# Attention scores: one product over 128 rows and 144 columns, or two products over 64 rows and 72 columns each

## The chip, the cores and the metric

The kernel runs on one core of a Trainium2 chip. The metric is the device time of one execution in microseconds, median of three. For the kernel before that is 1152.58 us (1152.16 to 1152.69).

## The reference

The program is pooled attention, then a dense mixture of four experts, then a gated block. Only the scores of the attention change; they are the product in the fifth line below.

```
q, k, v: (4 batches, 8 heads, 576 tokens, 64 dims)
k_p = k.reshape(B, H, 72, 8, D).mean(axis=3)          # 72 pooled keys per head
v_p = v.reshape(B, H, 72, 8, D).mean(axis=3)
scale = 1 / sqrt(64)
scores = scale * q @ k_p.T                            # per head: 576 x 64 by 64 x 72
attn = softmax(scores, axis=-1)                       # the kernel adds 1e-9 to the sum, as the reference does
x = attn @ v_p
x -> (2304, 512); out = sum over 4 experts of p_e * relu(x @ w1_e) @ w2_e
a, b = out @ g_w1, out @ g_w2;  result = ((a * b) @ g_w3) @ g_wout
```

## The kernel before

The 2304 tokens are cut into 18 tiles of 128, and three tiles make a block of 384. A batch has 576 tokens, so tile 4 and tile 13 lie across the border of two batches; `segments` cuts those two into halves of 64 tokens, and the other sixteen are whole.

Attention runs for each tile in steps written out by hand. `make_qT` turns q so that the 128 partitions hold the 64 dims of an even head and the 64 dims of the odd head next to it; there are four such pairs. `make_kT` turns the pooled keys the same way. To keep the two heads of a pair apart, the pooled keys are spread over twice the columns: a pair has 144 columns, the first 72 nonzero only in the even head's 64 rows, the last 72 only in the odd head's (the mask `mk` in `pool_k`). `scores` multiplies qT (the stationary operand, 128 rows by 128 tokens) with these 144 columns, pair by pair, so half of what TensorE multiplies is zero. Two PSUM banks take a tile: pairs 0 and 1 in the first, pairs 2 and 3 in the second. The data is f32, and one matmul of the program stands in the trace as two passes, each with its own weight load; a whole tile is 4 matmuls and 8 passes.

`exps` then takes one bank after the other: a maximum on VectorE (L516), a subtraction on VectorE (L522) and the exponential on ScalarE (L523). For the first two tiles it is instead a scaling on VectorE (L518) and one exponential per head on ScalarE (L520). `sums` and `normalise` follow, `attn_T` transposes the result on TensorE (L543), and `attend` (L558) multiplies with the pooled values into x, where the two heads of a pair go to output partitions 0 to 63 and 64 to 127.

Tiles 0 to 2 are done in a lead of fixed order, in which nothing else is there for TensorE. Tiles 3 to 17 are hooks between the units of the first expert (`g`, L174 to L176, three passes over 384 or 512 columns each). In that part the attention's steps share two PSUM banks in turn (`spare[:2]`): scores, transposes of the keys and of the probabilities, and the first two pairs of `attend`. A step waits until ScalarE and VectorE have read what was in the bank before. [...] After 181 us no attention is left.

Of the kernel before, what the change touches and what calls it, by code (L numbers as in the profile page):

```python
# [17 lines left out]
def fused_kernel(  # L18
# [16 lines left out]
    nc = tc.nc  # L35
    PSUM = bass.MemoryType.PSUM

    B, H, S, D = q.shape
    POOL = 8
    NK = S // POOL  # L40
    NT, DM = out.shape
    E, _, F = moe_w1.shape
    P = 128
# [10 lines left out]
    NP = H // 2  # L54
# [6 lines left out]
    def segments(t0, n):  # L61
        done = 0
        while done < n:
            b, s = divmod(t0 + done, S)
            step = min(n - done, S - s)
            yield done, step, b, s
            done += step
# [263 lines left out]
    with tc.manual_schedule():  # L331
# [16 lines left out]
        def bank(name):  # L348
            turn[0] += 1
            return spare[(turn[0] - 1) % len(spare)](name)  # L350
# [46 lines left out]
        in_t, kb_t, kT_t, vp_t, qT_t, sc_t, e_t, sm_t, at_t = {}, {}, {}, {}, {}, {}, {}, {}, {}  # L397
# [96 lines left out]
        W = 2 * NK  # L494
        G = H // 2

        def scores(t):
            qT = qT_t.pop(t)
            sc_t[t] = []
            for half in range(2):  # L500
                sc = bank("sc")
                for hp in range(2 * half, 2 * half + 2):
                    for off, n, b, s in segments(t * P, P):
                        nc.tensor.matmul(sc[off:off + n, (hp % 2) * W:(hp % 2 + 1) * W],  # L504
                                         qT[:, hp, off:off + n], kT_t[b][:, hp * W:(hp + 1) * W],
                                         start=True, stop=True)
                sc_t[t].append(sc)

        def exps(t):
            e = ap.tile([P, H, NK], F32, tag="e", name="e", bufs=3)  # L510
            mx = ap.tile([P, H], F32, tag="mx", name="mx")
            for half, sc in enumerate(sc_t.pop(t)):
                s3 = sc[:, :2 * W].rearrange("p (g j) -> p g j", j=NK)
                m = mx[:, half * G:(half + 1) * G]
                eh = e[:, half * G:(half + 1) * G]
                nc.vector.tensor_reduce(m, s3, axis=AX.X, op=ALU.max)  # L516
                if t < LEAD - 1:
                    nc.vector.tensor_scalar(m, m, -LOGIT, None, op0=ALU.mult)  # L518
                    for g in range(G):
                        nc.scalar.activation(eh[:, g], s3[:, g], AF.Exp, scale=LOGIT, bias=m[:, g:g + 1])  # L520
                else:
                    nc.vector.tensor_tensor(eh, s3, m.unsqueeze(2).broadcast_to([P, G, NK]), op=ALU.subtract)  # L522
                    nc.scalar.activation(eh, eh, AF.Exp, scale=LOGIT)  # L523
            e_t[t] = e
# [75 lines left out]
        def do_scores(t):  # L600
            return [(None, lambda: scores(t))]

        def do_exps(t):
            return [(None, lambda: exps(t))]
# [887 lines left out]
```

## Time and profile before

| | |
|---|---|
| median of 3 runs | 1152.58 us |
| the profiled execution's own time | 1151.8 us |
| its span, first to last instruction | 1150.0 us |
| TensorE busy | 1138.5 us, 99% |
| weight loads busy | 1031.7 us, 90% |
| VectorE busy | 795.9 us, 69% |
[...]

The chain that ended last is read backwards from the last instruction and says which engine's work fills the time. In the rows below, PE is TensorE's matmuls and PEld its weight loads. Matmuls are pipelined: a matmul row's own duration holds latency that the next one overlaps, so the cost of a pass is the distance from one start to the next, which the chain's rows give directly. "x8" means eight records merged into one row.

### The profile page before, as it was taken

How to read it: one execution, taken by the hardware profiler on the slowest of the kernel's cores; microseconds unless marked ns; L12 is line 12 of the kernel's file. 1: busy time of each engine (PE TensorE's matmuls, PEld its weight loads, DVE VectorE, ACT ScalarE, POOL GpSimd, SP SyncE). 2: the span in 40 equal slices, each digit the busy share in tenths (PEclk: the TensorE clock that was granted, in tenths of full speed). 3: DMA queues.
4: the chain of work that ended last, by engine and by line, in shares of the span. 5: the costliest groups of instructions: out<-in, count | busy, mean ns of one | idle time of the engine just before them, and what ended most of it. 6: DMA issues, size and time to landing. Idle time of an engine off the chain costs nothing.

```text
span 1150.0 us, 17113 instructions
## 1 busy us (share of the span) xinstructions
PE 1138.5 (99%) x5966; PEld 1031.7 (90%) x5966; DVE 795.9 (69%) x1464; ACT 369.8 (32%) x615; POOL 422.3 (37%) x393
## 2 busy tenths in 40 slices
PE   7999999999999999999999999999999999999998
PEld 6898888999989898989898989989889999999997
DVE  6867553767858598658689677877786675774554
ACT  4543433345413053504134421305353223230110
POOL 6974312423615156634335652515000111331211
PEclk9999999999999999999999999999999999999999
DMA  9865525345785825495954677785486075947341
GB/s 214 210 154 136 164 89 201 138 178 179 273 271 168 263 78 161 131 311 172 268 157 129 192 233 188 236 212 139 151 192 236 33 270 201 334 156 282 116 166 55
DMA packets 213766, 213.85 MB, mean 186 GB/s; under 512 B 88880, under 2 KB 169008, under 8 KB 213680
## 3 DMA queue, kind: packets, MB, share of 16 engines
q1 hardware_dynamic: 213392, 212.23, 59.7%
q8 instruction: 47, 0.77, 0.3%
q10 hardware_dynamic: 288, 0.52, 0.1%
q14 instruction: 39, 0.32, 0.1%
HBM read 140.87 MB, written 71.83 MB: 185 GB/s over the span
## 4 chain that ended last, share of the span: by engine, by line
PE 98%; DVE 1%; ACT 0%; issue 0%; DMA 0%; POOL 0%; DVEq 0%; ACTq 0%
PE g L176 18%; PE g L174 18%; PE g L175 18%; PE s L176 13%; PE s L174 13%; PE s L175 13%; PE sc L504 1%; PE x_ps L558 1%; PE at_ps L543 1%; DMA stxh<-in_k_dram 0%; DVE ap L419 0%; PE vp_ps L452 0%; PE kT_ps L432 0%; PE qT_ps L483 0%; ACT ap L520 0%
## 5 line engine op out<-in xcount | busy, mean ns | idle before, releaser
L958 DVE TENSOR_TENSOR plain<-s,plain 128x384 f32<-128x384 f32 x300 | 158.4, 554 | 83.6 <-PE s L176 34.9
L180 POOL TENSOR_TENSOR round<-x5l,round 128x768 fp32r<-128x768 f32 x60 | 112.0, 1866 | 271.5 <-ACT round L179 245.1
L176 PE MATMUL s<-xo,wl 128*128 128x384 f32 x624 | 208.6, 334 | 0.0
L174 PE MATMUL s<-xo,wh 128*128 128x384 f32 x624 | 208.6, 334 | 0.0
L175 PE MATMUL s<-xo,wh 128*128 128x384 f32 x624 | 208.5, 334 | 0.0
L174 PE MATMUL g<-w2l,round 128*128 128x512 f32 x522 | 204.8, 392 | 0.0
L176 PE MATMUL g<-w2h,round 128*128 128x512 f32 x522 | 203.8, 390 | 0.0
L175 PE MATMUL g<-w2h,round 128*128 128x512 f32 x522 | 203.5, 390 | 0.0
L175 PEld LDWEIGHTS s<-xo,wh 128*128 128x128 f32 x624 | 117.1, 188 | 0.5
L174 PEld LDWEIGHTS s<-xo,wh 128*128 128x128 f32 x624 | 117.1, 188 | 0.5
L176 PEld LDWEIGHTS s<-xo,wl 128*128 128x128 f32 x624 | 117.1, 188 | 0.0
L176 PEld LDWEIGHTS g<-w2h,round 128*128 128x128 f32 x522 | 98.0, 188 | 20.6
L174 PEld LDWEIGHTS g<-w2l,round 128*128 128x128 f32 x522 | 98.1, 188 | 20.0 <-issue 0.8
L175 PEld LDWEIGHTS g<-w2h,round 128*128 128x128 f32 x522 | 98.0, 188 | 19.4
L292 POOL TENSOR_TENSOR x5l<-x5l,x5h 128x256 uint32<-128x256 uint32 x80 | 60.4, 755 | 137.7 <-DVE x5h L291 134.2
L962 ACT ACTIVATE plain<-s 128x384 f32<-128x384 f32 x60 | 29.2, 487 | 230.8 <-PE s L176 226.6
L179 ACT ACTIVATE round<-x5l 128x768 fp32r<-128x768 f32 x60 | 50.8, 847 | 147.8 <-DVE x5l L1352 146.7
L180 POOL TENSOR_TENSOR round<-plain,round 128x768 fp32r<-128x768 f32 (+1 forms) x29 | 52.3, 1805 | 117.6 <-ACT round L179 78.6
L286 DVE TENSOR_SCALAR x5l<-x5h 128x256 uint32<-128x256 uint32 x80 | 50.0, 625 | 52.7 <-DMA gate<-x5l 28.6
L958 DVE TENSOR_TENSOR x5l<-s,plain 128x384 f32<-128x384 f32 x120 | 65.6, 555 | 24.4 <-PE s L176 17.8
L1190 ACT ACTIVATE plain<-plain 128x768 f32<-128x768 f32 x36 | 30.6, 849 | 112.0 <-DVE plain L958 112.0
L174 PE MATMUL g<-xl,round 128*128 128x384 f32 x192 | 66.1, 344 | 0.0
(240 smaller groups left out, 2207.3 us busy)
## 6 DMA issues: line engine op xcount, KB each, us to landing
xo<-keptx SPq DMA_DIRECT2D x42, 768.0 KB
raw<-in_moe_w_dram SPq DMA_DIRECT2D x64, 256.0 KB
keptx<-xo SPq DMA_DIRECT2D x12, 768.0 KB
x5h<-in_moe_w_dram SPq DMA_DIRECT2D x128, 64.0 KB
x5h<-in_moe_w_dram SPq DMA_DIRECT2D x32, 256.0 KB
ob<-acc SPq DMA_DIRECT2D x24, 256.0 KB
kept<-xo SPq DMA_DIRECT2D x8, 768.0 KB
xo<-kept SPq DMA_DIRECT2D x8, 768.0 KB
```

The costliest lines, as they stand in the source:

```text
L174: nc.tensor.matmul(ps, lh, rl, start=first, stop=False)
L175: nc.tensor.matmul(ps, lh, rh, start=False, stop=False)
L176: nc.tensor.matmul(ps, ll, rh, start=False, stop=last)
L179: nc.scalar.activation(hi, src, AF.Copy)
L180: (lo_eng or nc.vector).tensor_tensor(lo, src, hi.bitcast(F32), op=ALU.subtract)
L286: nc.vector.tensor_scalar(au, h, 0x7FFFFFFF, None, op0=ALU.bitwise_and)
L292: nc.gpsimd.tensor_tensor(au, au, l, op=ALU.add)
L504: nc.tensor.matmul(sc[off:off + n, (hp % 2) * W:(hp % 2 + 1) * W], qT[:, hp, off:off + n], kT_t[b][:, hp * W:(hp + 1) * W], start=True, st ...
L543: nc.tensor.transpose(pt[:NK, g * P:(g + 1) * P], e[:, half * G + g, :], ident)
L958: nc.vector.tensor_tensor(to, one, two, op=ALU.add)
L962: nc.scalar.activation(x, product(j, A11, B11), AF.Copy)
L1190: nc.scalar.activation(r, r, AF.Relu)
```

## The change

`scores` takes each head by itself: the head's own 64 rows of qT as the stationary operand and its own 72 nonzero columns of the spread keys. Even heads (rows 0 to 63) go to one bank, odd heads (rows 64 to 127) to the other, and the two alternate. Both banks are taken before the first matmul. `exps` reads 4 x 72 columns of a bank and writes them to every second head of e.

```diff
         def scores(t):
             qT = qT_t.pop(t)
-            sc_t[t] = []
-            for half in range(2):
-                sc = bank("sc")
-                for hp in range(2 * half, 2 * half + 2):
-                    for off, n, b, s in segments(t * P, P):
-                        nc.tensor.matmul(sc[off:off + n, (hp % 2) * W:(hp % 2 + 1) * W],
-                                         qT[:, hp, off:off + n], kT_t[b][:, hp * W:(hp + 1) * W],
-                                         start=True, stop=True)
-                sc_t[t].append(sc)
+            sc_t[t] = [bank("sc") for _ in range(2)]
+            for off, n, b, s in segments(t * P, P):
+                for hp in range(NP):
+                    for a, sc in enumerate(sc_t[t]):
+                        rows = slice(a * D, (a + 1) * D)
+                        nc.tensor.matmul(sc[off:off + n, hp * NK:(hp + 1) * NK], qT[rows, hp, off:off + n],
+                                         kT_t[b][rows, hp * W + a * NK:hp * W + (a + 1) * NK], start=True, stop=True)
 
         def exps(t):
...
             for half, sc in enumerate(sc_t.pop(t)):
-                s3 = sc[:, :2 * W].rearrange("p (g j) -> p g j", j=NK)
+                s3 = sc[:, :G * NK].rearrange("p (g j) -> p g j", j=NK)
                 m = mx[:, half * G:(half + 1) * G]
-                eh = e[:, half * G:(half + 1) * G]
+                eh = e[:, half::2]
```

On TensorE's queue, at tile 0 in the lead, before (sc_210 and sc_213 are the tile's two banks, qT_ps the transposes of q, the size is that of the output):

```order
L483 MATMUL qT_ps_204<-ident_83,stxh_98 128x128 x4
L504 MATMUL sc_210<-ap1_72,plain_70 128x144 x2
L504 MATMUL sc_213<-ap1_72,plain_70 128x144 x2
L483 MATMUL qT_ps_237<-ident_83,stxh_98 128x128 x4
L504 MATMUL sc_243<-ap1_72,plain_70 128x144 x2
L504 MATMUL sc_246<-ap1_72,plain_70 128x144 x2
```

The same place in the changed kernel (sc_210 and sc_211 are the two banks):

```order
L483 MATMUL qT_ps_204<-ident_83,stxh_98 128x128 x4
L504 MATMUL sc_210<-ap1_72,plain_70 128x72
L504 MATMUL sc_211<-ap1_72,plain_70 128x72
L504 MATMUL sc_210<-ap1_72,plain_70 128x72
L504 MATMUL sc_211<-ap1_72,plain_70 128x72
L504 MATMUL sc_210<-ap1_72,plain_70 128x72
L504 MATMUL sc_211<-ap1_72,plain_70 128x72
L504 MATMUL sc_210<-ap1_72,plain_70 128x72
L504 MATMUL sc_211<-ap1_72,plain_70 128x72
L483 MATMUL qT_ps_241<-ident_83,stxh_98 128x128 x4
```

There are twice as many matmuls with half the columns, and the first bank is complete only with the last matmul but one; before it was complete after the second of four.

At tile 7, behind `attend` of a block and ahead of the expert's second product (x_ps is attend's output, g2 the expert's), on TensorE before:

```order
L558 MATMUL x_ps_836<-ap1_72 64x192 x4
L504 MATMUL sc_843<-ap1_72 128x144 x2
L504 MATMUL sc_846<-ap1_72 128x144 x2
L174 MATMUL g2_518<-w2l_694,round_71 128x512
L175 MATMUL g2_518<-w2h_693,round_71 128x512
```

And in the changed kernel:

```order
L556 MATMUL x_ps_868<-ap1_72 64x192 x4
L504 MATMUL sc_875<-ap1_72 128x72
L504 MATMUL sc_876<-ap1_72 128x72
L504 MATMUL sc_875<-ap1_72 128x72
L504 MATMUL sc_876<-ap1_72 128x72
L504 MATMUL sc_875<-ap1_72 128x72
L504 MATMUL sc_876<-ap1_72 128x72
L504 MATMUL sc_875<-ap1_72 128x72
L504 MATMUL sc_876<-ap1_72 128x72
L174 MATMUL g2_534<-w2l_722,round_71 128x512
L175 MATMUL g2_534<-w2h_721,round_71 128x512
```

The neighbours stay as they were; only the scores between them are other instructions. (The lines behind the diff are two less in the changed kernel: L558 is L556 there.)

## Rows read from the trace of the kernel before

**Rows 1.** The page: span, busy time of two engines, the chain by line

```profile
span 1150.0 us, 17113 instructions
PE 1138.5 (99%) x5966; PEld 1031.7 (90%) x5966; DVE 795.9 (69%) x1464; ACT 369.8 (32%) x615; POOL 422.3 (37%) x393
...
PE 98%; DVE 1%; ACT 0%; issue 0%; DMA 0%; POOL 0%; DVEq 0%; ACTq 0%
PE g L176 18%; PE g L174 18%; PE g L175 18%; PE s L176 13%; PE s L174 13%; PE s L175 13%; PE sc L504 1%; PE x_ps L558 1%; PE at_ps L543 1%; DMA stxh<-in_k_dram 0%; DVE ap L419 0%; PE vp_ps L452 0%; PE kT_ps L432 0%; PE qT_ps L483 0%; ACT ap L520 0%
```

**Rows 2.** The chain in order of time, 11 to 128 us: start, length, what

```profile
11.41 0.97 PE sc L504 x4
...
12.40 0.47 DVE ap L516
...
15.02 0.50 ACT plain L488
...
15.56 1.25 PE sc L504 x8
16.81 2.60 PE vp_ps L452 x16
...
28.80 0.49 ACT round L689
...
38.86 1.20 PE sc L504 x16
40.06 0.38 PE g L174
40.44 0.18 PE g L175
...
47.41 0.98 PE sc L504 x8
48.39 0.23 PE g L174
...
63.63 2.75 PE x_ps L558 x32
66.38 1.18 PE sc L504 x8
...
96.27 1.18 PE sc L504 x8
...
126.14 0.98 PE sc L504 x16
127.12 0.43 PE g L174
127.54 0.23 PE g L175
```

**Rows 3.** Weight loads (PEld) at 38.3 to 40.5 us, in order of time

```profile
39.99 0.19 PEld L174 LDWEIGHTS g<-xl,round 128*128 128x128 f32 x1 [0.20 <-issue]
40.10 0.19 PEld L175 LDWEIGHTS g<-xh,round 128*128 128x128 f32 x1
```

**Rows 4.** What VectorE does between 30 and 116 us, in order of time

```profile
30.52 0.45 DVE L516 TENSOR_REDUCE ap<-sc 128x4 f32<-128x288 f32 x1
...
37.62 1.09 DVE L491 STREAM_TRANSPOSE ap<-stxl 128x512 f32<-128x512 f32 x1 [0.50 <-DMA stxl<-in_v_dram]
...
95.58 1.84 DVE L180 TENSOR_TENSOR xl<-x_ps,xh 128x384 fp32r<-128x384 f32 x3
...
115.83 0.46 DVE L516 TENSOR_REDUCE ap<-sc 128x4 f32<-128x288 f32 x1 [3.44 <-PE sc L504]
```

**Rows 5.** What TensorE waited for, 26 to 39 us (nothing after that)

```profile
PE kT_ps L432 <- POOL plain L424: 1.1, 2, 0.6
PE sc L504 <- DVE ap L491: 0.8, 1, 0.8
```

**Rows 6.** A stretch of the lead: busy time by engine, then PEclk, DMA share, GB/s

```profile
11.00:12.07 1.07, 1.07 (x5) 0.89 (x5) 0.08 (x1) 0.60 (x1) 0.62 (x1) 0.50 0.80 222
```

## The prediction

> **What bounds the kernel now.** I read the page first: TensorE is busy 99% of the span and fills 98% of the chain that ended last; the scores are 1% of that chain [rows 1]. So the time follows TensorE's queue, and what the scores take or leave there counts almost one to one. Then the chain in order of time, for the distances between starts. [...] Last the waits: behind the lead TensorE waits 1.1 and 0.8 us, all of it ahead of 39 us, and after that for nothing [rows 5].
>
> Two rows show what smaller products can do. The tiles on a batch border already use a stationary operand of 64 columns, and two such products run side by side: tile 13 has 16 passes of 144 columns in 0.98 us, 61 ns each, half of 122. x_ps does it too: 32 passes of 192 columns in 2.75 us, 86 ns against 162 [rows 2]. But going into or out of this split costs. Tile 7, straight behind x_ps, takes 1.18 us where tile 5 takes 0.98; the first g behind tile 13 takes 0.43 where the next takes 0.23, and behind tile 4 0.38 where the next takes 0.18; the first g behind the unsplit tile 5 takes a plain 0.23 [rows 2]. So each change between whole array and split array costs 0.20 us. Rows 3 show of what: nothing is loaded ahead across the change, so the old products run empty and then the first weights load in the open. These loads start at 39.99 and 40.10, one right behind the other, so loading 128 columns takes 0.11 us.
>
> **The change, part by part.** *The passes.* A whole tile becomes 16 passes of 72 columns. [...] Each pass now needs its own load of 128 columns (64 rows deep), twice as many loads as before, and a load takes 109 ns [rows 3]. [...] No row shows two loads into different row halves, so I bound it. Below: a pair costs only its matmuls, 62 ns, the tile 0.50 us. Above: no two loads overlap at all, 16 x 109 = 1.74 us. The nearest row is the column split: tile 13 loads 16 operands of 64 columns, each about half of 109 ns, 16 x 55 = 0.88 us if in turn, and its 0.98 us would allow that as well as loads in pairs. I take loads in pairs, each behind the matmul before it, so 109 ns a pair: 8 x 109 = 0.87 us in place of 0.98, a gain of 0.10 us a whole tile. Tiles 5 to 12 and 14 to 17 stand where TensorE never waits: 12 x 0.10 = -1.25 us.
>
> *The changes of split.* A product on 64 rows is a split array like the one on 64 columns. No row shows a split by rows; the bounds are 0 and the 0.20 us of the column split, and I take 0.20, the only row there is. Of the 12 tiles, nine (5, 6, 8, 9, 11, 12, 14, 15, 17) stand between whole-array work and get two new changes each; tiles 7, 10 and 16 come behind x_ps, which is a change already, and get one new one, on the way out. 21 x 0.20 = +4.2 us. Tile 13 was split by columns like x_ps ahead of it; now it is split both ways, so one more change on entry, +0.15 (its 64-column load is shorter). Its 32 passes of 72 columns pair to 16 x 62 = 0.99 us, against 0.98.
>
> [...]
>
> *Tiles 3 and 4.* Between 28.80 and 38.86 the chain goes over ScalarE and VectorE and not over TensorE [rows 2]; TensorE's waits cover what tile 3 gains or loses, and VectorE reads tile 3's scores only at 30.52 [rows 4]. Tile 4 was split already. Both 0.
>
> *The lead.* Tile 0's scores are on the chain: four passes (the first bank), the maximum at 12.40, then the exponentials, and behind them on ScalarE's queue the copy of tile 2's q (L488, 15.02), for which tile 2's scores wait until 15.56 [rows 2]. Now the first bank is done only at the end of all passes. [...] I take +0.3, between 0 and 0.8.
>
> *Waits and the other engines.* VectorE's instruction on the first bank waits longer, up to 0.5 us, and blocks what is queued behind it, the expert's round<-g. VectorE has waits of up to 3.44 us there already without TensorE ever waiting for it [rows 4, 5]: 0. Both banks must be free at the start, the second 0.5 us earlier than before. Tight behind x_ps only: VectorE frees the second bank with the first of three instructions that begin at 95.58 and last 0.61 each, 96.19, and tile 10's scores stand on the chain from 96.27 [rows 2, 4]. 0, at most 4 x 0.1. Writing every second head moves the same 288 elements: 0, at most 36 x 0.05 us on VectorE, which is busy 69% [rows 1].
>
> *Sum.* -1.25 + 4.2 + 0.15 + 0.3 = +3.4 us on the profiled execution's 1151.8, so 1155.2. That execution lies 0.78 us under the median of 1152.58; carried over, **1156.0 us**.
>
> **The rivals.**
>
> *A. Split loads do not overlap (slower still).* For it: no row shows two 64-row loads at once, and the weights may come by one path. Against: the column split runs 61 ns a pass with its loads. If in turn, a whole tile is 1.74 us, +0.77 x 12 = 9.2; tile 13 and tile 4 32 loads of 55 ns, 1.76, +0.78 each; the lead about +2 (tile 0's first bank some 1.3 later, tile 2 0.77 longer); the changes 4.35: +17, 1169 to 1170. If instead halves overlap but a load can't hide behind its own half's matmul, a pair is 109 + 62 = 171 ns, a tile 1.37: +0.39 x 12 + 1.7 + 1 + 4.35 = +12, 1164.
>
> *B. No drain for rows (not slower).* For it: rows 3 show it for columns alone, and whole-array products load ahead of each other. Against: the row split is the same kind of change. Then -1.25 and the lead's +0.3: 1151.6.
>
> *C. Loads are no limit: pairs at matmul speed (faster).* For it: half the columns, and two products side by side, as tile 13 shows. Against: rows 3, a load is 109 ns. A tile 0.50 us, -0.48 x 12 = -5.8. Without changes of split and with a lead of +0.2: 1147; with them (4.35) 1151.4. It is faster than the bound below as long as a change costs under 0.15 us (5.6 less 2.3, over 22 changes).
>
> [...]
>
> *D. The two heads do not run side by side at all:* two passes in turn, bound by loads: the same 1.74 us as A, counted with it.
>
> **How the numbers follow.** Forecast 0.54 (its own range 1154.0 to 1158.5: the lead, 0.15 to 0.22 us a change). A with D 0.22, half at 1164 and half at 1170. B 0.13. C without changes 0.07, with them 0.04. Range: 1151 leaves out C's 0.07 and some of B below; 1167 leaves out A's upper half, 0.11. Inside 0.2% (2.3 us, 1150.3 to 1154.9; about what a measurement of this kernel can tell from no change) lie B, C with changes, and the edge of the forecast: 0.18. Faster 0.08, slower 0.74.
>
> **What would show it.** In the changed profile: pairs of sc weight loads a few ns apart and the next pair 0.11 us later (forecast), 0.06 (C), all singly at 0.11 (A); a whole tile near 0.9 us without its edges; the first g behind every scores block 0.20 us longer than the next, and the first scores 0.2 us behind the last g's end. [...] The prediction is wrong if g's first row behind tile 5 stays at 0.23 (B), or if the chain's sc share grows past 2.5% (A).

## The result, and the profile after

The changed kernel takes 1160.67 us (six runs, 1159.76 to 1161.30), against 1152.52 us for the kernel before on the same chip (1151.88 to 1153.30). That is 8.1 us more, a ratio of 1.0070 (95% interval 1.0057 to 1.0083). It is slower, as forecast, and inside the range, but the forecast was +3.4, and 1160.67 us lies above the 1154.0 to 1158.5 that the forecast gave itself. The execution profiled here is the slowest of the six, 1161.3 us; against the profile of before, which was its fastest, that makes +9.5, so the terms below add up to a little more than the medians differ by.

The page of the changed kernel, the lines that answer to [rows 1], and the row of the granted clock in 40 slices of 29 us:

```profile
span 1159.5 us, 17433 instructions
PE 1149.5 (99%) x6126; PEld 1036.5 (89%) x6126; DVE 795.2 (69%) x1464; ACT 369.9 (32%) x615; POOL 422.9 (36%) x393
...
PEclk6999999999999999999999999999999999999999
...
PE g L174 18%; PE g L176 18%; PE g L175 18%; PE s L174 13%; PE s L176 13%; PE s L175 13%; PE sc L504 2%; PE at_ps L541 1%; PE x_ps L556 1%; PE vp_ps L452 0%; DMA stxl<-in_k_dram 0%; DMA stxl<-in_v_dram 0%; PE warm L631 0%; POOL stxh L421 0%; DVE ap L419 0%; PE kT_ps L432 0%
```

Two things are seen. The scores' share of the chain went from 1% to 2%. And the first slice has a clock of 6 tenths, where the page of the kernel before has 9 (90% or more):

```profile
PEclk9999999999999999999999999999999999999999
```

The chain in order of time (start, length, what) shows the lead; these lines answer to [rows 2]:

```profile
11.46 1.97 PE sc L504 x16
13.43 0.45 DVE ap L514
...
16.52 1.98 PE sc L504 x16
18.50 5.32 PE vp_ps L452 x16
23.82 1.28 PE warm L631 x6
...
28.86 1.56 ACT ap L547 x3
...
45.67 1.03 PE sc L504 x28
46.70 0.38 PE g L174
```

The same stretch of the kernel before, the lines that [rows 2] left out, and its last x_ps:

```profile
19.41 0.66 PE warm L633 x6
...
22.07 1.57 ACT ap L549 x3
...
181.06 2.73 PE x_ps L558 x16
```

Tile 4's scores start at 45.67 instead of 38.86, 6.8 us later, and all of it is there at 28.86 against 22.07, where ScalarE copies the turned probabilities out of at_ps (L547, before L549). Piece by piece: tile 2's scores start 0.96 later (16.52 for 15.56) and last 0.73 longer; vp_ps takes 5.32 for 2.60, +2.72; the fillers and transposes behind it (`warm`, `at_ps`), up to that copy, 28.86 - 23.82 = 5.04 for 22.07 - 19.41 = 2.66, +2.38. Sum 6.79. None of vp_ps, `warm` and `at_ps` was changed. They take twice as long because the granted clock did not rise: it is 0.50 from 16 to 28 us, where it was 1.00. The next two fences are windows of the stretch, of the kernel before and of the changed one (window, length, busy time of PE, PEld, DVE, ACT, POOL with counts, then PEclk, DMA share, GB/s):

```profile
8.60:12.07 3.47, 3.05 (x13) 2.87 (x14) 1.50 (x2) 1.47 (x3) 1.58 (x4) 0.51 0.96 216
12.07:16.00 3.93, 2.65 (x21) 2.43 (x21) 3.44 (x9) 2.78 (x13) 3.46 (x9) 1.00 1.05 255
```

```profile
8.60:12.07 3.47, 3.02 (x17) 2.67 (x18) 1.55 (x2) 1.45 (x3) 1.46 (x4) 0.50 0.99 216
12.07:16.00 3.93, 3.93 (x34) 3.47 (x32) 1.16 (x4) 1.86 (x10) 3.54 (x8) 0.50 1.01 240
...
28.00:32.00 4.00, 3.66 (x27) 2.54 (x27) 1.83 (x3) 2.57 (x5) 0.98 (x1) 0.93 0.32 80
```

Before, the granted clock goes from 0.50 to 1.00 at 12.07, during tile 0's scores. After, it stays at 0.50 until 28.56, while TensorE is hardly idle (busy 18.8 of the 19.4 us from 8.60 to 28.00).

The steady part, on the chain of the changed kernel:

```profile
54.05 1.05 PE sc L504 x16
55.09 0.43 PE g L174
...
73.56 1.04 PE sc L504 x16
74.61 0.43 PE g L174
...
134.54 0.96 PE sc L504 x28
135.50 0.43 PE g L174
...
190.36 2.73 PE x_ps L556 x16
```

A block and the g behind it are read together, since the change of split shows in that g. Tile 5: 1.05 + 0.43 = 1.48 where [rows 2] has 0.98 + 0.23 = 1.21, so +0.27. Tile 7: 1.47 where it was 1.18 + 0.23, so +0.06. Tile 13: 1.39 where it was 0.98 + 0.43, so -0.02. Tile 4: 1.03 + 0.38 where it was 1.20 + 0.38, so -0.17. With nine tiles of tile 5's kind and three of tile 7's that is 9 x 0.27 + 3 x 0.06 - 0.02 - 0.17 = +2.4. The last x_ps of the attention confirms it: 190.36 against 181.06 is +9.30, 6.81 of it there when tile 4 starts, so +2.5 from there on.

Inside tile 6, windows of the scores' line alone (PE and PEld busy with the count of records in the window, PEclk, DMA share, GB/s) show the loads that answer to [rows 3]:

```profile
62.34:62.36 0.02, 0.02 (x2) 0.02 (x2) 1.00 0.00 0
62.36:62.44 0.08, 0.08 (x2) 0.08 (x2) 1.00 0.18 26
62.44:62.46 0.02, 0.02 (x2) 0.02 (x4) 1.00 0.00 0
```

Two loads start at 62.34 and none follows until two more at 62.45: pairs, one for each half of the rows, 0.11 us apart. TensorE's waits from 26 to 200 us (engine, line, releaser: total, times, longest) answer to [rows 5]; the longest is tile 4's, 0.8 as before, and behind it there is none to 200 us:

```profile
PE sc L504 <- DVE ap L491: 0.8, 1, 0.8
```

### The profile page after: what moved, and what is told of

It reads as the page before. It is cut to its first block, busy times and chain, and to the rows that moved or that the text cites. A ratio compares the mean times of both kernels' runs of the same rounds, so it can differ in the third digit from the quotient of the medians.

```text
span 1159.5 us, 17433 instructions
## 1 busy us (share of the span) xinstructions
PE 1149.5 (99%) x6126; PEld 1036.5 (89%) x6126; DVE 795.2 (69%) x1464; ACT 369.9 (32%) x615; POOL 422.9 (36%) x393
## 4 chain that ended last, share of the span: by engine, by line
PE 97%; POOL 1%; DMA 1%; ACT 0%; DVE 0%; issue 0%; SPq 0%; ACTq 0%; POOLq 0%; DVEq 0%
PE g L174 18%; PE g L176 18%; PE g L175 18%; PE s L174 13%; PE s L176 13%; PE s L175 13%; PE sc L504 2%; PE at_ps L541 1%; PE x_ps L556 1%; PE vp_ps L452 0%; DMA stxl<-in_k_dram 0%; DMA stxl<-in_v_dram 0%; PE warm L631 0%; POOL stxh L421 0%; DVE ap L419 0%; PE kT_ps L432 0%
## 5 line engine op out<-in xcount | busy, mean ns | idle before, releaser
L174 PEld LDWEIGHTS g<-w2l,round 128*128 128x128 f32 x522 | 98.1, 188 | 20.5 <-issue 0.6
L175 PEld LDWEIGHTS g<-w2h,round 128*128 128x128 f32 x522 | 98.0, 188 | 19.4
```

Source lines behind the costliest of these rows:

```text
L174: nc.tensor.matmul(ps, lh, rl, start=first, stop=False)
L175: nc.tensor.matmul(ps, lh, rh, start=False, stop=False)
```

## The experiments

All kernels compute the whole result; the fillers named below are products that nobody reads. Each difference is against the kernel before on the same chip.

**Lead or steady part: tiles 0 to 2 apart from the rest.** Two kernels that together are the change:

```diff
+        def by_head(t):
+            return t >= LEAD      # first kernel: only tiles 3 to 17 by head
+            return t < LEAD       # second kernel: only tiles 0 to 2 by head
...
+        def scores(t):
+            (scores_heads if by_head(t) else scores_pairs)(t)
```

> Tiles 0 to 2 with the pair products of before, tiles 3 to 17 with one product per head. Theory (the loss of 8 us is two things: +2.5 us from changes of split behind the lead, +6.8 us from the low clock, 0.50 from 8.08 to 28.56 us, in the lead): the clock is back at 1.00 by about 12 us, the lead is as before, and 1155.0 us remain (1154.5 to 1155.7). Rival (what is lost lies behind the lead, the lead only shows it): 1159 to 1161.

> Tiles 0 to 2 with one product per head, all others with the pair products of before. Theory: clock 0.50 until about 28.5 us again and +6.8 us, 1159.3 us (1158.5 to 1160). Rival 1 (the low clock was not of the change but of that execution): 1152.5 to 1153.1. Rival 2 (the first bank's late end, forecast at +0.3 to +0.8, and nothing more): 1152.8 to 1153.3, clock as before.

Measured: 1155.29 (ten runs), +2.2, ratio 1.0020 (1.0010 to 1.0029), for tiles 3 to 17 alone; 1158.72 (four runs), +5.7, ratio 1.0048 (1.0033 to 1.0063), for the lead alone. The two add to 7.9 of the 8.1: two thirds and more of the loss is in the lead. With tiles 0 to 2 back to pairs the chain has vp_ps in 2.60 us again, and with the lead alone by head in 5.32 (first line and second):

```profile
16.77 2.60 PE vp_ps L452 x16
```

```profile
18.15 5.32 PE vp_ps L452 x16
```

But the clock of the first kernel was not back "by about 12 us". Its window from 12 to 16 us has a mean of 0.68:

```profile
12.00:16.00 4.00, 3.83 (x22) 3.61 (x21) 2.28 (x8) 2.73 (x11) 3.59 (x8) 0.68 1.06 276
```

It rose at 14.55, during tile 1's scores, with the lead's instructions those of the kernel before, where it rose at 12.07. So the moment of the rise differs between executions of the same instructions.

The first kernel also has a wait that the changed one has not. Its chain at tile 6:

```profile
55.53 0.97 ACT ap L565 x2
...
56.55 1.11 PE sc L519 x14
```

Two passes of the first even head had started at 56.06; the other 14 stood until ScalarE had read the second bank, and tile 6 cost 0.95 instead of 0.27. Banks that must both be free at the start thus cost 0.7 us in this profile.

**Tile 0 alone.** Only tile 0 takes pairs (`return t > 0`).

> Only tile 0 with the pair products of before, all others with one product per head. Theory (it is tile 0's scores, the first dense work behind the waits for the keys, that lift the clock): clock 1.00 from about 12 us to the end, 1155.0 to 1156.0 us. Rival (any split-by-rows stretch in the lead lets the clock fall or holds it): the clock falls again behind tiles 1 and 2, at 14 to 18 us, and 1157 to 1160 us.

Measured: 1156.17 (eight runs, 1155.35 to 1160.00), +3.1, ratio 1.0031 (1.0021 to 1.0042), just above the theory's range. In the profiled execution, 1155.74 us, the clock rises at 11.68, during tile 0's scores, and stays up. Three of the eight runs (1157.27, 1158.26, 1160.00) lie in the rival's range, and no trace shows where they lost their time. So tile 0 by pairs gives most of the lead's loss back in most executions; that its scores alone lift the clock is not shown, since in the kernel with the whole old lead it rose only during tile 1's. The chain and the windows of this kernel:

```profile
15.14 1.12 PE sc L519 x16
16.26 2.75 PE vp_ps L452 x16
```

```profile
8.60:12.20 3.60, 3.59 (x18) 3.41 (x19) 1.29 (x3) 1.47 (x3) 1.52 (x4) 0.57 0.90 218
12.20:16.00 3.80, 2.59 (x39) 2.28 (x37) 3.25 (x9) 3.08 (x13) 3.41 (x8) 1.00 1.08 262
```

Tiles 1 and 2 are by head here, and 16 passes take 1.12 us, not 1.98.

**Short passes without the split by rows.** Each head over all 128 rows (the other head's half of the spread keys is zero):

```diff
-    nc.tensor.matmul(sc[off:off + n, hp * NK:(hp + 1) * NK], qT[rows, hp, off:off + n],
-                     kT_t[b][rows, hp * W + a * NK:hp * W + (a + 1) * NK], start=True, stop=True)
+    nc.tensor.matmul(sc[off:off + n, hp * NK:(hp + 1) * NK], qT[:, hp, off:off + n],
+                     kT_t[b][:, hp * W + a * NK:hp * W + (a + 1) * NK], start=True, stop=True)
```

> Half the columns without the split by rows: 16 passes a tile with the whole 128 rows of q as stationary operand and the head's own 72 columns (the other head's rows are zero there), two banks as in the changed kernel. Theory (a load of 128 columns takes 0.109 us and nothing here is side by side): a whole tile 16 x 0.109 = 1.74 us, no longer first g behind it, +0.77 x 12 = 9.2 us behind the lead, about +2 in the lead with the clock up at about 12 us: 1163.5 us (1162 to 1165). Rival 1 (loads are no limit): 62 ns a pass, 0.99 us a tile, 1152.5 to 1153.5. Rival 2 (it is the 72 columns, not the split, that hold the clock down): the clock stays at 0.50 to about 28 us here too, another +6 to +7 us, 1169 to 1171.

Measured: 1173.56 (four runs), +20.5, ratio 1.0177 (1.0160 to 1.0194). The chain of this kernel:

```profile
22.54 5.12 PE vp_ps L452 x16
...
58.44 1.74 PE sc L518 x16
60.18 0.28 PE g L174
```

In the steady part 16 passes start 0.108 us apart on average, 1.74 us, and the g behind them is back to 0.28: no change of split. A tile costs 0.81 more than before, and the fifteen tiles together 12.1, where the theory had counted twelve tiles, 9.2; that is why the whole lies above the second rival's range too. So a load of 128 columns bounds a pass at 0.11 us, with 128 rows (0.108 from start to start) as with 64 (pairs 0.11 apart), and the split into row halves is what lets two run at once. In the lead vp_ps is slow here too, without any split. The second rival is right for the lead: the clock stayed at 0.50 until 31.6 us without any split, behind 72-column passes with loads of 128 columns in place of 144-column ones.

**Even heads first, then odd ones** (tiles 3 to 17):

```diff
-    for hp in range(NP):
-        for a, sc in enumerate(sc_t[t]):
+    for a, sc in enumerate(sc_t[t]):
+        for hp in range(NP):
```

> As e1 (lead of before), but from tile 3 on a tile's four even heads come first and then its four odd heads, in place of alternating. Theory (a pair costs one load time because the two row halves load and multiply side by side; products in the same half cannot): no pairs any more, 16 x 0.109 = 1.74 us a tile, +0.85 on each of 12 tiles and +0.8 on tile 13 against e1, so 13 us above the kernel before (11 to 14). Rival (TensorE pairs them whatever the order, or the pairs bring nothing): as e1, 2 us above the kernel before.

Measured: 1161.83 (four runs), +8.7, ratio 1.0079 (1.0065 to 1.0093). Neither theory. Windows of the scores' line in tile 6 (busy PE and PEld with counts):

```profile
57.19:57.70 0.51, 0.50 (x4) 0.50 (x5) 1.00 0.83 253
57.70:58.04 0.34, 0.34 (x9) 0.34 (x9) 1.00 0.95 198
58.04:58.60 0.56, 0.56 (x10) 0.56 (x8) 1.00 0.78 230
```

At first one half runs alone, a pass every 0.11 us as the theory had it. From 57.71 the odd half's first load and matmul start, with three passes of the even half still to come, and the two halves run side by side; then the odd half ends alone. A block is 1.35 us, between the 0.84 of alternating heads and 16 passes in turn (both from first to last start).

**A change of split by itself.** A whole-array transpose of the identity into unused columns, in the middle of each whole tile from 3 on, so that it leaves and enters the split once more:

```diff
+    if hp == NP // 2 and n == P:
+        nc.tensor.transpose(sc_t[t][0][:, 384:384 + P], ident, ident)
```

> As e1, with one whole-array transpose of the identity (128 columns, into unused columns of the first bank) in the middle of each whole tile's scores from tile 3 on. Theory (each change between whole and split array costs 0.20 us): two more changes and one pass of 0.11 us for each of 12 tiles, 12 x 0.51 = 6.1 us on top of e1, 8.3 us above the kernel before (7.3 to 9). Rival (the 0.20 us are a matter of the neighbours g and x_ps, not of the split): 12 x 0.11 = 1.3 on top of e1, 3.5 us above.

Measured: 1159.49 (four runs), +6.4, ratio 1.0056 (1.0042 to 1.0070), 4.2 above the kernel without the transpose. The chain at tile 5:

```profile
47.43 0.60 PE sc L521 x8
48.03 0.26 PE sc L518
48.29 0.60 PE sc L521 x8
48.89 0.43 PE g L174
```

The block with the two extra changes is 1.46 us where it was 1.05: +0.41. Less a transpose of 0.11 us (`warm` has six in 0.66), two changes cost 0.30, 0.15 each. Twelve tiles at 0.41 make 4.9; tile 6's bank wait of 0.7, which this profile does not have, takes it to the 4.2 measured. So a change of split by rows does cost time: the result lies below the theory's 6.1 and well above the rival's 1.3, and between short passes a change is 0.15 rather than 0.20.

**The clock without the change: more fillers in the kernel before.** 20 instead of 14 at the start, and four behind each of the first three key transposes:

```diff
+    for _ in range(WARM[c] if b == 0 else 0):
+        nc.tensor.transpose(pw[:, :P], ident, ident)
...
-        W0, W1, W2 = 14, 6, 6
+        W0, W1, W2 = 20, 6, 6
+        WARM = (4, 4, 4, 0, 0)
```

> The kernel before with more whole-array transposes of the identity in TensorE's waits for the first keys: 20 in place of 14 at the start, and 4 behind each of the first three key transposes. Theory (the clock falls at 8.66 us because TensorE is mostly idle from 4.7 to 8.7, and everything to 12.07 runs at half speed for it): the clock stays at 1.00 from 5 us on, q's transposes and tile 0's scores take half the time, 1.0 to 1.3 us less than the kernel before. Rival (something else ends last in the lead, or the fillers delay the keys): within 0.4 us of the kernel before, or slower.

Measured: 1152.00 (eleven runs), -1.1, ratio 0.9990 (0.9981 to 0.9999). As expected, but the interval ends just short of no change. Ten of the eleven runs have a recorded mean clock of 1.000; the eleventh, 1154.76 us, has 0.997.

**The same fillers in the changed kernel.**

> The changed kernel with the same fillers as e7. Theory (products per head do not lift a low clock, but do not lower a high one either, as tiles 1 and 2 of e4 show): the clock never falls in the lead, the +6 us of the lead are gone, and what remains is the +2.2 us of e1 less about 1: 1 to 1.5 us above the kernel before. Rival (products per head lower the clock as well when tile 0 is one): the clock falls at 12 to 16 us and stays low to about 28: 5 to 8 us above the kernel before.

Measured: 1159.69 (five runs), +6.6, ratio 1.0060 (1.0046 to 1.0074). My theory, that a clock up before tile 0 would leave only about 1 us of the lead's loss, fell. Windows of this kernel:

```profile
9.00:17.00 8.00, 6.12 (x68) 5.03 (x67) 6.01 (x15) 5.52 (x20) 5.66 (x13) 1.00 1.01 253
17.00:24.00 7.00, 7.00 (x30) 5.80 (x29) 4.72 (x10) 1.80 (x4) 5.20 (x8) 0.51 0.79 188
```

The scores of tiles 0 to 2 run at a granted clock of 1.00, with a wait of 1.6 us for tile 2's q ahead of the last:

```profile
PE sc L507 <- ACT plain L491: 1.6, 1, 1.6
```

Behind them, in vp_ps (4.75 us), the clock falls: 0.51 on average from 17 to 24 us. The wait alone does not separate the cases: the kernel before with more fillers has it too, 1.2 us, and its profile has no fall (1.00 from 9 to 24 us).

**That wait filled**, with ten more fillers ahead of tile 2's scores (`+ warm(10) + do_scores(2)`).

> e8 (products per head everywhere, fillers between the keys) with ten more whole-array transposes of the identity between the scores of tile 1 and tile 2, where TensorE waits 1.55 us in e8. Theory (the clock fell there because a wait of 1.5 us stood between stretches of split products, which count for little; with the wait filled it stays up): the clock stays at 1.00 through the lead, tile 0's pooled values (vp_ps) take 2.6 us again and not 4.75, 1.0 to 2.0 us above the kernel before. Rival (split products alone, or the 72 by 72 products of vp_ps behind them, lower it whatever stands between): the clock falls at 16 to 20 us again, 5 to 7 us above.

Measured: 1158.15 (five runs), +5.0, ratio 1.0048 (1.0036 to 1.0061). In the profiled execution the clock now stays up through the lead (1.00 from 9 to 24 us, vp_ps 2.8 us), as the theory said, but the sum fell: the gain is lost again behind it. TensorE's waits from 20 to 60 us:

```profile
PE sc L507 <- DVE ap L494: 2.2, 1, 2.2
PE g L174 <- DVE xl L180: 1.2, 1, 1.2
```

VectorE and the transfer for tile 4's q (DMA stxl on the chain until 38.9) now come later than TensorE needs them, and the clock drops once more around tile 4 (0.72 on average from 40 to 46 us, the first g there 0.62 instead of 0.38).

**By head only where the array is split anyway**, in the border tiles 4 and 13, with the fillers:

```diff
+        def by_head(t):
+            return len(list(segments(t * P, P))) > 1
```

> e7 (pair products, fillers between the keys), with products per head only in the border tiles 4 and 13, which are split anyway. Theory (there the changes of split are paid already): e7's gain of 1.1 us and at most 0.2 more, 1.0 to 1.4 us under the kernel before. Rival (the second bank, needed at once, makes TensorE wait, 0.5 us as at tile 6 of e1): 0.5 to 0.8 under.

Measured: 1153.44 (eleven runs, 1151.11 to 1156.16), +0.2, ratio 1.0001 (0.9992 to 1.0010), so neither figure came. In the trace the two tiles gain 0.17 and 0.02 as expected, but the profiled execution (1155.92 us) has the fall of the clock at vp_ps (0.57 on average from 16 to 24 us), although its lead is instruction for instruction that of the kernel before with more fillers. TensorE's timeline, of the kernel with border tiles by head and then of the kernel before with more fillers:

```profile
16.00 4.79 PE L455 MATMUL vp_ps<-stxl,ident 72*72 72x192 f32 x16 [0.25 <-DMA stxl<-in_v_dram]
```

```profile
15.74 2.79 PE L455 MATMUL vp_ps<-stxl,ident 72*72 72x192 f32 x16 [0.17 <-DMA stxl<-in_v_dram]
```

The same 16 passes behind a wait of 0.2 us take 4.79 or 2.79 us. So the clock may fall at that place with the lead's scores all by pairs, in some executions and not in others, and the fall in the changed kernel with fillers can't be put on products by head alone. What lets it fall there is open. The low clock of the changed kernel's own lead did not come and go like this: the runs with tile 0 by head and no added fillers (six of the changed kernel, four with the lead alone, four over 128 rows) lie within 1.6 us of each other in each kernel, and all three traces have the slow vp_ps, 5.1 to 5.3 us.

## Why the prediction was right in direction and short in size

The direction has the reason that was given for it: the steady part alone, where the changes of split cost more than the passes gain, is 2.2 us slower. The size has not. The measured 1160.67 us is inside the range because the range left room for rival A, at 1164, and it was not A that happened: that it came out inside is luck.

- *Passes bound by their loads, two halves side by side:* right in kind. Pairs of loads start 0.11 us apart, and a whole tile takes 0.84 us from its first to its last start; eight passes of 144 columns took 0.86, so most of the 0.10 forecast as a gain is not seen: the second pair's matmuls start 0.17 us behind the first's, not 0.11. A load of 128 columns takes 0.11 us from one start to the next, with 64 rows (62.34 to 62.45) and with 128 ([rows 3]). The forecast's 122 ns for a pass of 144 columns are tile 5's 0.98 us over eight passes, its 162 ns vp_ps's 2.60 us over sixteen ([rows 2]); its 62 ns for 72 columns are the author's estimate, about half of the 122.
- *Changes of split, 21 x 0.20:* right, somewhat large. From the last score pass to the next load is 0.20, as forecast, but tiles with two changes cost +0.27 net for a forecast of 0.30, those with one +0.06 for 0.10, and tile 13 -0.02 for 0.16. At tile 13 the entry does cost 0.10: its first pass starts 0.42 us behind the last start of x_ps, where it was 0.32, and its passes and the way out are 0.12 shorter. Whether the 0.10 is the change or the second bank, which VectorE frees only 0.09 before, is not shown. The experiment with the transpose has a cost for rows as well, 0.15 us a change.
- *Tiles 3 and 4, 0:* tile 4 gains 0.17.
- *Steady sum:* +3.1 forecast, +2.5 in the profile, +2.2 (about 1.2 to 3.3) in the kernel that has only this part, the bank wait at tile 6 included.
- *The lead, +0.3 (0 to 0.8):* this is the term that failed. The 0.3 is the author's estimate, and no run shows it; in its place the runs show 6.8 in the profile and 5.7 in the kernel that has only this part. The first maximum came at 13.43, where it was 12.40, and tile 4's scores 6.8 later. The clock of 0.50 up to 12.07 ([rows 6]), with 1.00 behind it, belongs to one execution of the old instructions. With the changed ones it stayed at 0.50 until 28.56, and with it went vp_ps, the fillers and the transposes, which the diff doesn't touch. Tile 0 by pairs gives most of it back in most executions (+3.1 in all); 72-column passes without a split lose it just the same.
- *Waits and other engines, 0:* right in this kernel. VectorE's wait for the scores grew, and TensorE didn't notice. The bound of 0.1 for a bank was wrong, though: 0.7 us in the kernel with the old lead.
- *The rivals.* A and D: seen only where one half has nothing to alternate with. B fell with the 0.20 us behind every block; C with the 0.11 us between loads.

What stays open: why short passes in the lead keep the clock low, and what sets the moment of its rise; why it falls at vp_ps in some executions with fillers; why the bank wait of tile 6 shows in some orders and not in others.

## What to carry to other kernels

Halving the work of a small product saved next to nothing here (0.84 us a whole tile from first to last start, for 0.86), because its weight load is the bound (a pair of loads every 0.11 us); count loads, and changes between whole and split array, before multiplications. Where the array is split already, the new split was not dearer (the border tiles: 0.17 and 0.02 us less in the trace), but the time of the kernel did not show that gain. A row of the clock holds for the execution that it was taken from (12.07 and 14.55 us for the same lead), and less still for other instructions: where a change makes passes shorter in a stretch in which the clock has yet to rise, put the whole of that stretch at the low clock (here 0.50, and 5.32 us for a vp_ps of 2.60) into the range, the untouched instructions too.

## What was not expected of the hardware

- The two row halves ran as separate streams, out of program order across halves: with even heads first, the first odd pass of tile 6 starts at 57.71 with three even ones, earlier in the program, still to start. It starts 0.51 us behind the first even pass (57.20); what holds it until then is not shown.
- The granted clock stayed at 0.50 from 8.1 to 28.6 us of nearly unbroken matmuls (18.8 of the 19.4 us from 8.60 to 28.00), 16 passes of 72 by 72 (vp_ps, 5.32 us) among them; with 128 rows and short passes it stayed there until 31.6 us.
- The record of the clock missed a stretch: the kernel with only the lead changed has a recorded mean of 1.000, though its vp_ps takes 5.32 us there as well.
